# A linear-attention kernel with a feed-forward stage: four visits whose cross-half products go to PSUM banks of their own

## The chip, the core and the metric

The kernel runs on one core of a Trainium2 chip. TensorE (PE in the profile) multiplies matrices into PSUM, an accumulator of 8 banks, each of 512 float32 values on each of 128 partitions. VectorE (DVE), ScalarE (ACT) and GpSimd (POOL) do the element-wise work, and SyncE (SP) issues most of the loads and stores; GpSimd issues the weights' loads. The metric is the device time of one execution, in microseconds. Lower is better.

## What is computed

The first stage is causal linear attention with a decay. There are 4 batches, 8 heads, 768 positions and 64 channels; `lam` holds one decay per head. Position i attends to j <= i with weight `lam**(i-j)`, in blocks of 64 with a state between them:

```python
for b in range(nb):
    intra = einsum(qb, kb) * Dmask           # lam**(i-j) where i >= j
    intra = einsum(intra, vb)
    inter = einsum(qb * lam**(pos+1), kv_state)
    out[block] = intra + inter
    kv_state = lam**block * kv_state + einsum(kb * lam**(block-1-pos), vb)
```

The second stage takes these outputs as 3072 rows x of 512 and computes `h = x @ w_in` (512 to 2048), `g = h * cos(h)` and `g @ w_out` (2048 to 512). All inputs and the output are float32; the matmuls are done in bfloat16.

## The kernel before

**Blocks, visits and pairs.** The 3072 rows are 24 visits of 128 positions, each two halves of 64. Two visits of two batches make a pair. The first two pairs (visits 0 to 3, `SPANS`) are done at the start in another layout (`add_span`). Pairs 2 to 11 go through `prepare`, `add_scores` and `add_stretch`. Names such as q4 or v5 are loads for the visit of that number, so the loads of visits 4 and 5 are those of the third pair.

**One pair.** q and v are scaled by powers of `lam` (L341, L349), k is cast (L345). q and k are transposed, on TensorE for pair 2 and by a DMA for later pairs (L377). `scores` (L419) multiplies k with q into two banks ps_s, and VectorE masks them into s_m (L424). `update` (L431) adds up k times v into ps_kv, and VectorE and ScalarE make the running state from it (L437, L442). `values` and `values_carried` (L480, L508) make the output in two banks ps_o, one for each visit: first the "cross" products, in which half 0 of the array's rows works on visit 1 and half 1 on visit 0, then the "straight" ones, in which half s works on visit s, then the products with the carried state. `values_out` (L516) copies a bank to xT, the input of the feed-forward stage.

**Why there is a drain.** [...]between cross and straight products each half changes its bank. Where the scores of the next pair are put between the two groups, a small copy on VectorE (`turn`, L493) tells that the first group is over. Pairs 3 to 6 have their scores elsewhere (`ALONE = [3, 4, 5, 6]`), so behind pairs 2, 3, 4, 5 and 11 there is nothing to put between, and TensorE drains:

```python
def values_carried(_):
    if not more:
        nc.tensor.drain()
```

**The feed-forward stage.** `add_ffn` works on tiles of 4, 2, 2, 2, 2, 2, 2, 4 and 4 visits. For each of 16 column blocks f, `hidden` (L705) makes ps_h from xT and w_in, ScalarE its cosine (L711), VectorE the product g (L717). `project` (L749) multiplies g with w_out into ps_f, ScalarE copies that to o_sb (L763), and SyncE stores it.

**Order.** A planner in the kernel (`Planner`) puts all tasks in an order from costs that are written in the code, takes PSUM banks as they come free in its plan, and the program is recorded in that order. On the chip each engine goes through its own instructions in this fixed order and waits by semaphores. The order of loads is written out by hand (`ORDER`); `add_load` and `add_w` make each load wait for an earlier one where the list changes between weights and inputs:

```python
ORDER = "q0 k0 q1 k1 v0 v1 i0 i1 i2 i3 i4 i5 o0 o1 o2 q4 q5 k4 k5 o3"
deps = [kept[-3 if soft else -2]] if at and (names[at - 1][0] in "io") != soft else []
```

Here i0 to i5 are the pieces of w_in (`W_IN = [2, 2, 2, 4, 4, 2]` blocks f), o0 to o3 those of w_out. So q4 waits for the landing of o1, v4 for that of k5, and o3 for that of q4. i3 waits in addition for VectorE's first masked scores of the second span (`w_late`). GpSimd issues i0, i1 and i2 first, then scales k of the second span, then issues i3 and the rest. Until the main stage begins TensorE has filler matmuls (`keep_awake`).

Of the kernel before, what the change touches and what calls it, by code (L numbers as in the profile page):

```python
# [18 lines left out]
SPANS = 2  # L19
# [5 lines left out]
ATT = 0.95  # L25
LOAD_US = 1.22
ALONE = [3, 4, 5, 6]


QK = [{"q": ("DVE", "DVE"), "k": ("DVE", "DVE")}, {"q": ("DVE", "DVE"), "k": ("POOL", "POOL")}]  # L30
# [111 lines left out]
def kernel(  # L142
# [12 lines left out]
    P = 128  # L155
# [132 lines left out]
    def add_load(n, name, src, prio, deps=()):  # L288
        b, c = where(n)

        def emit(_):
            t = loads.tile([P, H, D], F32, tag=name, name=name)
            live[name, n] = t
            return start(nc.sync, t, src[b, :, c * P:(c + 1) * P, :].transpose([1, 0, 2]), deps)

        issue_t[name, n], load_t[name, n] = dma("SP", LOAD_US, 0.85, emit, prio, deps, get=name, lat=1.0)
        return load_t[name, n]

    w_t, w_late = {}, []

    def add_w(which, c, prio, deps=()):
        def emit(_):
            if which == "in":
                a, z = sum(W_IN[:c]) * P, sum(W_IN[:c + 1]) * P
                i = start(nc.gpsimd, w_in_sb[:, :, a:z], w_in_src[:, :, a:z], deps)
                if c == 3:

                    tc.add_manual_dep(i.ins, w_late[0].ins.ins.name, mybir.DependencyInfo(
                        mybir.DependencyClass.Sync, mybir.DependencyReason.DATA), reason="lines of instructions first")
                return i  # L310
            a, z = c * KF // WCH, (c + 1) * KF // WCH
            return start(nc.gpsimd, w_out_sb[:, a:z, :], w_out_src[:, a:z, :], deps)

        part = W_IN[c] / 4 if which == "in" else 1.0
        early = which == "in" and c < 3
        _, w_t[which, c] = dma("POOL", 2.68 * part, 0.8, emit, -2000.0 if early else prio, deps,
                               lat=1.2)
        return w_t[which, c]
# [151 lines left out]
    def add_stretch(pr):  # L470

        n0 = 2 * pr
        g, c = divmod(pr, NB)
        pa = lambda part: prio_attn(n0, part)
        tile_i, j0 = tile_of(n0)

        def value(s, half):
            m, o = halves[half], live["o", n0 + s]
            for h in range(H):
                yield lambda h=h: nc.tensor.matmul(  # L480
                    o[halves[h % 2], h // 2, m], lhsT=live["v_s", n0 + s][m, h, :], rhs=live["s_m", n0 + s][m, h, :],
                    start=(s != half and h < 2), stop=True, skip_group_check=True)

        def values(t):
            for s in range(2):
                live["o", n0 + s] = bank(t.bank[s], [P, NP, P], F32, "ps_o")
            for x, y in zip(value(1, 0), value(0, 1)):
                x()
                y()

        def turn(_):

            live["turn", pr] = nc.vector.tensor_copy(spare[D:D + 1, 0:1], live["o", n0][D:D + 1, NP - 1, D:D + 1])  # L493

        def values_carried(_):
            if not more:
                nc.tensor.drain()
            for x, y in zip(value(0, 0), value(1, 1)):
                i = x()
                y()  # L500
                if ("turn", pr) in live:
                    tc.add_manual_dep(i.ins, live.pop(("turn", pr)).ins.name, mybir.DependencyInfo(
                        mybir.DependencyClass.Sync, mybir.DependencyReason.DATA), reason="row halves in turn")
            for half in range(0 if c else 1, 2):
                S = live["S", pr, 0] if half else live["S", pr - 1, 1]
                for h in range(H):
                    for s, r in enumerate(halves):
                        nc.tensor.matmul(live["o", n0 + s][halves[h % 2], h // 2, halves[half]], lhsT=S[r, h, :],  # L508
                                         rhs=live["qkT", pr][r, 0, h, halves[half]],
                                         start=False, stop=True, skip_group_check=True)  # L510

        def values_out(_, s, e):
            if ("xT", tile_i) not in live:
                live["xT", tile_i] = work.tile([P, KD, 4 * P], BF16, tag="xT", name="xT")
            j = j0 + s
            (nc.vector.tensor_copy if e == "DVE" else nc.scalar.copy)(  # L516
                live["xT", tile_i][:, :, j * P:(j + 1) * P], live.pop(("o", n0 + s)))

        deps = [So[n0], So[n0 + 1], Uo[pr, 0], Uo.get((pr - 1, 1)) if c else None]
        more = pr + 1 < NBLK // 2 and pr + 1 not in ALONE  # L520
        v1 = pl.add("PE", 4 * QUART + SW, deps, values, pa(0.5), banks=2)
        chain = [v1]
        if more:
            nxt = list(add_scores(pr + 1, pa(0.5)))
            for t in nxt:
                v1.deps += [d for d in t.deps if d not in nxt]
            chain += nxt
        if more:
            deps = deps + [pl.add("DVE", 0.12, [v1], turn, pa(-9.0))]
        v2 = v12[pr] = pl.add("PE", (12 if c else 8) * QUART + (0.0 if more else 0.28), deps, values_carried, pa(0.5))  # L530
        chain.append(v2)
        v1.bank_frees = []
        for s in range(2):
            e = "DVE" if pr == SPANS and s == 0 else "ACT"
            Vo[n0 + s] = [pl.add(e, 0.65, [v2] + ([h_last[tile_i - 2]] if tile_i >= 2 else []), partial(values_out, s=s, e=e),
                                 pa(0.0 if e == "DVE" else 0.6))]
            v1.bank_frees.append(Vo[n0 + s])
            So[n0 + s].frees = [v2]
            v_head[n0 + s].frees = [v2]
        qkT_head[pr].frees = [v2]  # L540
        if (pr + 1, 1) in Uo:
            Uo[pr + 1, 1].deps.append(v2)
        for x, y in zip(chain, chain[1:]):
            x.then = y
            y.deps.append(x)
# [4 lines left out]
    def add_span(x):  # L550
# [77 lines left out]
        for hp in range(2):  # L628
            eq, ek = QK[x]["q"][hp], QK[x]["k"][hp]
            a = pl.add(eq, us[eq], [load_t["q_f", "sp", x]], partial(prep, name="q", hp=hp, e=eq), pa(-0.9 + 0.1 * hp))  # L630
            kt.append(pl.add(ek, us[ek], [load_t["k_f", "sp", x]], partial(prep, name="k", hp=hp, e=ek), pa(-0.9 + 0.1 * hp)))
            if x:
                w_t["in", 3].issue.deps.append(kt[hp])
            outs = []
            for name, src in (("qT", a), ("kT", kt[hp])):
                e = OUTS[x][name][hp]
                t = pl.add("PE", MM(P, 4), [src, s_first if name == "kT" else None], partial(transposes, name=name, hp=hp), pa(-0.5 + 0.1 * hp), banks=1)
                outs.append(pl.add(e, 0.58 if e == "ACT" else 0.42, [t], partial(transposes_out, name=name, hp=hp, e=e), pa(-0.5 + 0.1 * hp)))
                t.bank_frees = [[outs[-1]]]
            s1 = pl.add("PE", 0.42, outs, partial(scores, hp=hp), pa(0.1 + 0.1 * hp), banks=2)  # L640
            if x and hp == 0:

                spans[0]["values"].deps.append(s1)
                s_first = s1
            so[hp] = [pl.add("DVE", 0.69, [s1], partial(scores_out, hp=hp, i=i), pa(0.1 + 0.1 * hp + 0.05 * i)) for i in range(2)]
            s1.bank_frees = [[t] for t in so[hp]]
            if x and hp == 0:
                w_late.append(so[hp][0])

        u = pl.add("PE", 0.42, v_t + kt + [spans[0].get("carried")], update, pv(0.1), banks=1)  # L650
        Uo_sp[x] = [pl.add(e, 0.4 if e == "ACT" else 0.42, [u], partial(update_out, h=h, e=e), pv(0.1))
# [37 lines left out]
    def add_ffn(i):  # L689
# [4 lines left out]
        for f in range(KF):  # L694
            gate[f] = []
            blocks = [(0, 2), (2, 4)] if i == 0 and f < SPLIT else [(0, nb)]
            for b0, b1 in blocks:
# [16 lines left out]
                def gated(_, f=f, at=at, n=n):  # L714
                    if ("g", i) not in live:
                        live["g", i] = work.tile([P, KF, 4 * P], BF16, tag="g", name="g")
                    nc.vector.tensor_mul(live["g", i][:, f, at], live.pop(("h", i, f, at.start))[:, :n],  # L717
                                         live.pop(("c", i, f, at.start))[:, :n])

                h = pl.add("PE", MM(n, 4), [x for m in range(n0 + b0, n0 + b1) for x in Vo[m]] + [w_t["in", next(c for c in range(len(W_IN)) if f < sum(W_IN[:c + 1]))]],  # L720
                           hidden, pr, banks=1)
# [2 lines left out]
                h.bank_frees = [[d]]  # L724
                a.frees = [d]
                gate[f].append(d)
                h_last[i] = h
                if i == 0:
                    hid.append(h)
# [58 lines left out]
    for at, name in enumerate(names):  # L788
        which, n = name[0], int(name[1:])
        soft = which in "io"  # L790
        deps = [kept[-3 if soft else -2]] if at and (names[at - 1][0] in "io") != soft else []
        if name == "o3":
            deps = [load_t["q_f", 2 * SPANS]]
        if soft:
# [6 lines left out]
    idle = pl.add("SETUP", 0.0, [], None, -1e9, banks=1)  # L801
    for x in range(SPANS):
        add_span(x)
    w_t["in", 3].issue.deps += w_late
    add_span_state()
    for pr in range(SPANS, NBLK // 2):
        prepare(pr)
# [8 lines left out]
        add_ffn(i)  # L816
    for f in range(2, SPLIT):
        hid[2 * f].deps.append(spans[1]["carried"])
    closing.deps.append(v12[SPANS])
    first_sum.deps += Vo[2 * SPANS]  # L820
    lead_end = hid[2 * SPLIT]
# [55 lines left out]
```

## Time and profile before

| what | value |
|---|---|
| three runs | 205.86, 206.45 (median), 206.87 us |
| profiled run | 206.59 us, span of the core 204.8 us |
| PSUM to xT copy on ScalarE, 128x512 (L516) | 589 ns each, x19 |
| product g on VectorE, 128x256 and 128x512 (L717) | 503 ns mean, x148 |
| q, k and v loads of 256 KB, issue to landing | 3.8, 4.3, 4.7 us (median) |
| w_out pieces of 512 KB, issue to landing | 12.1 us (median) |

The span runs from the first to the last instruction of the profiled execution, and all times in the trace count from its start. In rows of a timeline the first number is the start, the second the length of the merged stretch, and "x32" how many instructions it holds; the bracket gives the idle time before it and what ended that. Matmuls overlap, so the lengths of neighbouring rows on TensorE can overlap too; distances between starts are the safer measure. A few matmul records are missing, which shows as a gap of one matmul's length.

### The profile page before, as it was taken

Reading aid. Unit: us, or ns where it says so; the run is one execution under the profiler, and the core shown is the slowest. Engines: PE = TensorE matmul, PEld = TensorE weight load, DVE = VectorE, ACT = ScalarE, POOL = GpSimd, SP = SyncE. Lnnn points to the kernel's source line nnn. Section 1 sums busy time; section 2 is a strip of 40 time slices with the busy share of each in tenths; the row PEclk is TensorE's granted clock in tenths of the full one; section 3 lists DMA queues with packets and bytes.
Section 4 is the critical chain, followed back from the end, with each engine's and each line's share of the span. In section 5 each row is a group of like instructions: output and inputs, shape, how many; then the busy total and the mean of one; then the engine's idle time right before and its main releaser. Section 6 shows DMA issues by size and latency. Waiting matters only on the chain.

```text
span 204.8 us, 5936 instructions
## 1 busy us (share of the span) xinstructions
PE 195.6 (95%) x2457; PEld 117.6 (57%) x2485; DVE 113.6 (55%) x221; ACT 119.2 (58%) x232; POOL 64.8 (32%) x85
## 2 busy tenths in 40 slices
PE   6999999999999999999999999999999999999993
PEld 2467444547747848666658666755454444444463
DVE  2887783347953947559467664735687444444001
ACT  5978771128837868466649586645778555354120
POOL 5865004064345362616364443436300000000000
PEclk9999999999999999999999999999999999999999
DMA  4999999999989998999999889989700110111112
GB/s 128 317 190 196 199 202 214 187 205 232 213 214 231 259 213 202 209 201 251 216 270 155 204 183 215 246 202 268 133 0 6 51 51 0 51 54 51 51 71 82
DMA packets 96906, 33.94 MB, mean 166 GB/s; under 512 B 84336, under 2 KB 93936, under 8 KB 96880
## 3 DMA queue, kind: packets, MB, share of 16 engines
q1 hardware_dynamic: 89376, 28.78, 62.0%
q0 software_dynamic: 7360, 4.72, 16.3%
q8 instruction: 19, 0.31, 0.6%
q10 hardware_dynamic: 144, 0.07, 0.1%
q14 instruction: 7, 0.06, 0.1%
HBM read 27.27 MB, written 6.29 MB: 164 GB/s over the span
## 4 chain that ended last, share of the span: by engine, by line
PE 76%; DMA 14%; SPq 3%; POOL 2%; issue 2%; DVE 1%; ACT 0%; POOLq 0%; ACTq 0%
PE ps_f L749 35%; PE ps_h L705 34%; DMA w_out_sb<-in_moe_w_out_dram 6%; DMA v_f<-in_v_dram 3%; DMA sp_f<-in_k_dram 3%; SPq L266 3%; PE ps_o L480 2%; DMA k_f<-in_k_dram 2%; PE ps_kv L431 2%; PE ps_o L508 1%; PE ps_s L419 1%; POOL w_in_sb L266 1%; POOL k_sp L564 1%; DVE v_s L349 0%; POOL w_out_sb L266 0%
## 5 line engine op out<-in xcount | busy, mean ns | idle before, releaser
L717 DVE TENSOR_TENSOR g<-ps_h,cos 128x256 bf16<-128x256 f32 (+1 forms) x148 | 73.0, 503 | 51.7 <-ACT cos L711 50.7
L711 ACT ACTIVATE cos<-ps_h,halfpi 128x256 f32<-128x256 f32 (+1 forms) x148 | 75.8, 539 | 31.3 <-PE ps_h L705 30.9
L705 PE MATMUL ps_h<-xT,w_in_sb 128*128 128x256 bf16 (+1 forms) x587 | 91.4, 304 | 0.6 <-issue 0.5
L749 PE MATMUL ps_f<-w_out_sb,g 128*128 128x512 bf16 (+2 forms) x393 | 88.5, 362 | 2.2 <-issue 1.4
L705 PEld LDWEIGHTS <-w_in_sb 128*128 128x128 bf16 x592 | 57.1, 98 | 31.2 <-issue 0.6
L749 PEld LDWEIGHTS <-g 128*128 128x128 bf16 x416 | 38.5, 98 | 35.7
L763 ACT COPY o_sb<-ps_f 128x512 f32<-128x512 f32 (+1 forms) x24 | 13.8, 574 | 29.8 <-PE ps_f L749 29.5
L341 POOL TENSOR_TENSOR qk<-q_f,q_scale 128x512 bf16<-128x512 f32 x19 | 19.7, 1045 | 34.5 <-DMA q_f<-in_q_dram 21.8
L349 POOL TENSOR_TENSOR v_s<-v_f,v_scale 128x512 bf16<-128x512 f32 x19 | 19.6, 1044 | 21.6 <-DMA v_f<-in_v_dram 19.2
L516 ACT CAST xT<-ps_o 128x512 bf16<-128x512 f32 x19 | 10.3, 589 | 11.4 <-PE ps_o L508 8.9
L424 DVE TENSOR_TENSOR s_m<-ps_s,mask 128x512 bf16<-128x512 f32 x20 | 12.9, 684 | 3.3 <-PE ps_s L419 3.0
L345 POOL CAST qk<-k_f 128x512 bf16<-128x512 f32 x18 | 11.0, 614 | 5.8 <-DMA k_f<-in_k_dram 5.7
L437 DVE TENSOR_TENSOR sum<-sum,ps_kv 128x512 f32<-128x512 f32 x15 | 10.2, 683 | 0.8
L442 ACT CAST S<-sum 128x512 bf16<-128x512 f32 x15 | 9.0, 616 | 0.8 <-DVE sum L437 0.7
L480 PEld LDWEIGHTS <-v_s 64*64 64x64 bf16 x320 | 4.3, 106 | 5.0 <-issue 4.4
L763 DVE COPY o_sb<-ps_f 128x256 f32<-128x256 f32 (+1 forms) x2 | 0.7, 358 | 11.2 <-PE ps_f L749 11.2
L480 PE MATMUL ps_o<-s_m,v_s 64*64 64x64 bf16 x320 | 6.4, 198 | 0.5
L837 PE MATMUL ps_idle<-blank 128*128 128x512 f32 (+2 forms) x8 | 5.3, 814 | 1.6 <-DVE blank L209 1.6
L588 DVE TENSOR_TENSOR s_m_sp<-ps_s,mask_sp 128x512 bf16<-128x512 f32 x8 | 5.1, 684 | 1.0 <-PE ps_s L583 1.0
L431 PE MATMUL ps_kv<-v_s,qk 64*64 64x64 bf16 x288 | 4.7, 194 | 0.4 <-DVE v_s L349 0.3
L266 POOL DMA_DIRECT2D w_in_sb<-in_moe_w_in_dram x6 | 4.6, 774 | 1.7 <-DVE s_m_sp L588 1.7
L679 POOL CAST S<-sum 128x512 bf16<-128x512 f32 x1 | 0.6, 607 | 13.0 <-DVE sum L676 13.0
(70 smaller groups left out, 79.3 us busy)
## 6 DMA issues: line engine op xcount, KB each, us to landing
q_f<-in_q_dram SPq DMA_DIRECT2D x20, 256.0 KB, 3.8
k_f<-in_k_dram SPq DMA_DIRECT2D x20, 256.0 KB, 4.3
v_f<-in_v_dram SPq DMA_DIRECT2D x20, 256.0 KB, 4.7
out_dram<-o_sb SPq DMA_DIRECT2D x19, 256.0 KB, 2.4
w_out_sb<-in_moe_w_out_dram POOLq DMA_DIRECT2D x4, 512.0 KB, 12.1
out_dram<-o_sb SPq DMA_DIRECT2D x9, 128.0 KB, 3.8
sp_f<-in_q_dram SPq DMA_DIRECT2D x2, 512.0 KB, 5.0
sp_f<-in_k_dram SPq DMA_DIRECT2D x2, 512.0 KB, 6.0
```

Source lines behind the costliest of these rows:

```text
L266: i = queue.dma_start(out=o, in_=x)
L341: vec[e].tensor_mul(new_qk()[:, 0, :, s], live.pop(("q_f", 2 * pr + s)), q_scale[:, c, :].unsqueeze(2).to_broadcast([P, H, D]))
L345: (nc.scalar.copy if early else nc.gpsimd.tensor_copy)(new_qk()[:, 1, :, s], live.pop(("k_f", 2 * pr + s)))
L349: vec[e].tensor_mul(live["v_s", 2 * pr + s], live.pop(("v_f", 2 * pr + s)), v_scale[:, c, :].unsqueeze(2).to_broadcast([P, H, D]))
L424: nc.vector.tensor_mul(t, live["s", pr][s], mask.unsqueeze(1).to_broadcast([P, H, D]))
L480: yield lambda h=h: nc.tensor.matmul(o[halves[h % 2], h // 2, m], lhsT=live["v_s", n0 + s][m, h, :], rhs=live["s_m", n0 + s][m, h, :], sta ...
L516: (nc.vector.tensor_copy if e == "DVE" else nc.scalar.copy)(live["xT", tile_i][:, :, j * P:(j + 1) * P], live.pop(("o", n0 + s)))
L705: nc.tensor.matmul(t[:, :n], lhsT=w_in_sb[:, kd, f * P:(f + 1) * P], rhs=live["xT", i][:, kd, at], start=(kd == 0), stop=(kd == KD - 1))
L711: nc.scalar.activation(c[:, :n], live["h", i, f, at.start][:, :n], AF.Sin, bias=halfpi)
L717: nc.vector.tensor_mul(live["g", i][:, f, at], live.pop(("h", i, f, at.start))[:, :n], live.pop(("c", i, f, at.start))[:, :n])
L749: nc.tensor.matmul(live["f", i, j, piece][:, :width], lhsT=live["g", i][:, f, j * P:(j + 1) * P], rhs=w_out_sb[:, f, part], start=(f == 0) ...
L763: (nc.scalar.copy if eng == "ACT" else nc.vector.tensor_copy)(o[:, :width], live["f", i, j, piece][:, :width])
```

## The change

It has three parts.

1. In pairs 3, 4, 5 and 11 (`APART`) the cross products go to two further banks, ps_x, and the drain is left out. ScalarE copies each ps_x bank to SBUF (`cross_out`), and the output of each visit leaves in two halves: the half with no cross product as a copy on ScalarE, the other as a sum of ps_o and the copied cross product on VectorE (`halves_out`). The pair takes four banks.
2. q4 waits for VectorE's product of block f = 13 of tile 0 instead of o1's landing, and v4 for k4's landing instead of k5's.
3. i2, the third piece of w_in, is issued by GpSimd behind k's scaling instead of ahead of it, and i3 no longer waits for the masked scores.

The core of the diff:

```diff
+APART = [3, 4, 5, 11]
...
-        def value(s, half):
-            m, o = halves[half], live["o", n0 + s]
+        def value(s, half, o=None):
+            m = halves[half]
+            o = live["o", n0 + s][:, :, m] if o is None else o
...
-                    start=(s != half and h < 2), stop=True, skip_group_check=True)
+                    start=(apart or s != half) and h < 2, stop=True, skip_group_check=True)
...
+            if apart:
+                cross = live["cross", pr] = [bank(i, [P, NP, D], F32, "ps_x") for i in t.bank[2:]]
-            for x, y in zip(value(1, 0), value(0, 1)):
+            for x, y in zip(value(1, 0, cross[0]), value(0, 1, cross[1])):
...
-            if not more:
+            if not more and not apart:
                 nc.tensor.drain()
...
+            if s == half:
+                nc.scalar.copy(x, o)
+            elif half or c:
+                nc.vector.tensor_add(x, o, live["cross_f", pr][half])
...
+            nc.scalar.copy(live["cross_f", pr][half], live["cross", pr][half])
...
-        v1 = pl.add("PE", 4 * QUART + SW, deps, values, pa(0.5), banks=2)
+        v1 = pl.add("PE", 4 * QUART + SW, deps, values, pa(0.5), banks=2 + 2 * apart)
...
-                w_t["in", 3].issue.deps.append(kt[hp])
+                w_t["in", 2].issue.deps.append(kt[hp])
...
-    w_t["in", 3].issue.deps += w_late
...
+        if name == f"q{2 * SPANS}":
+            deps = []
+        if name == f"v{2 * SPANS}":
+            deps = [load_t["k_f", 2 * SPANS]]
...
+                if i == 0 and f == KF - 3:
+                    pace.append(d)
...
+    issue_t["q_f", 2 * SPANS].deps += pace
```

In the built program the order on TensorE is the same up to pair 3; from there some groups of ps_h and ps_f change places around the visits. SyncE's order changes only from the loads of pair 8 on, where some stores stand one or two places earlier or later; on GpSimd only the third piece moves.

More of the change, by code (lines that the diff above doesn't have):

```diff
@@ L293, in emit @@
             live[name, n] = t
-            return start(nc.sync, t, src[b, :, c * P:(c + 1) * P, :].transpose([1, 0, 2]), deps)
+            i = start(nc.sync, t, src[b, :, c * P:(c + 1) * P, :].transpose([1, 0, 2]), deps)
+            if (name, n) == ("q_f", 2 * SPANS):
+                tc.add_manual_dep(i.ins, pace[0].ins.ins.name, mybir.DependencyInfo(
+                    mybir.DependencyClass.Sync, mybir.DependencyReason.DATA), reason="order of loads")
+            return i
         issue_t[name, n], load_t[name, n] = dma("SP", LOAD_US, 0.85, emit, prio, deps, get=name, lat=1.0)
         return load_t[name, n]
-    w_t, w_late = {}, []
+    w_t, pace = {}, []
     def add_w(which, c, prio, deps=()):
@@ L304, in emit @@
                 a, z = sum(W_IN[:c]) * P, sum(W_IN[:c + 1]) * P
[L305 to L310, printed above, removed]
+                return start(nc.gpsimd, w_in_sb[:, :, a:z], w_in_src[:, :, a:z], deps)
             a, z = c * KF // WCH, (c + 1) * KF // WCH
@@ L475, in add_stretch @@
         tile_i, j0 = tile_of(n0)
-        def value(s, half):
-            m, o = halves[half], live["o", n0 + s]
+        def value(s, half, o=None):
+            m = halves[half]
+            o = live["o", n0 + s][:, :, m] if o is None else o
             for h in range(H):
                 yield lambda h=h: nc.tensor.matmul(
-                    o[halves[h % 2], h // 2, m], lhsT=live["v_s", n0 + s][m, h, :], rhs=live["s_m", n0 + s][m, h, :],
-                    start=(s != half and h < 2), stop=True, skip_group_check=True)
+                    o[halves[h % 2], h // 2], lhsT=live["v_s", n0 + s][m, h, :], rhs=live["s_m", n0 + s][m, h, :],
+                    start=(apart or s != half) and h < 2, stop=True, skip_group_check=True)
         def values(t):
@@ L486, in values @@
                 live["o", n0 + s] = bank(t.bank[s], [P, NP, P], F32, "ps_o")
-            for x, y in zip(value(1, 0), value(0, 1)):
+            cross = [None, None]
+            if apart:
+                cross = live["cross", pr] = [bank(i, [P, NP, D], F32, "ps_x") for i in t.bank[2:]]
+            for x, y in zip(value(1, 0, cross[0]), value(0, 1, cross[1])):
                 x()
@@ L517, in values_out, with halves_out, cross_out @@
                 live["xT", tile_i][:, :, j * P:(j + 1) * P], live.pop(("o", n0 + s)))
+        def halves_out(_, s, half):
+            if ("xT", tile_i) not in live:
+                live["xT", tile_i] = work.tile([P, KD, 4 * P], BF16, tag="xT", name="xT")
+            o, i = live["o", n0 + s][:, :, halves[half]], (j0 + s) * P + half * D
+            x = live["xT", tile_i][:, :, i:i + D]
+            if s == half:
+                nc.scalar.copy(x, o)
+            elif half or c:
+                nc.vector.tensor_add(x, o, live["cross_f", pr][half])
+            else:
+                nc.vector.tensor_copy(x, live["cross_f", pr][half])
+        def cross_out(_, half):
+            live.setdefault(("cross_f", pr), {})[half] = toks.tile([P, NP, D], F32, tag=f"cross{half}", bufs=1, name=f"cross{half}")
+            nc.scalar.copy(live["cross_f", pr][half], live["cross", pr][half])
         deps = [So[n0], So[n0 + 1], Uo[pr, 0], Uo.get((pr - 1, 1)) if c else None]
         more = pr + 1 < NBLK // 2 and pr + 1 not in ALONE
-        v1 = pl.add("PE", 4 * QUART + SW, deps, values, pa(0.5), banks=2)
+        apart = pr in APART
+        v1 = pl.add("PE", 4 * QUART + SW, deps, values, pa(0.5), banks=2 + 2 * apart)
         chain = [v1]
@@ L529, in add_stretch @@
             deps = deps + [pl.add("DVE", 0.12, [v1], turn, pa(-9.0))]
-        v2 = v12[pr] = pl.add("PE", (12 if c else 8) * QUART + (0.0 if more else 0.28), deps, values_carried, pa(0.5))
+        v2 = v12[pr] = pl.add("PE", (12 if c else 8) * QUART + (0.0 if more or apart else 0.28), deps, values_carried, pa(0.5))
         chain.append(v2)
         v1.bank_frees = []
+        if apart:
+            after = [v2] + ([h_last[tile_i - 2]] if tile_i >= 2 else [])
+            copies = [pl.add("ACT", 0.42, after, partial(halves_out, s=s, half=s), pa(0.6)) for s in range(2)]
+            moved = [pl.add("ACT", 0.42, [v1], partial(cross_out, half=half), pa(0.55)) for half in range(2)]
+            sums = [pl.add("DVE", 0.4, after + [moved[1 - s]], partial(halves_out, s=s, half=1 - s), pa(0.0 if pr == SPANS else 0.59 - 0.01 * s)) for s in range(2)]
+            for s in range(2):
+                Vo[n0 + s] = [copies[s], sums[s]]
+            v1.bank_frees = [Vo[n0], Vo[n0 + 1], [moved[0]], [moved[1]]]
         for s in range(2):
+            So[n0 + s].frees = [v2]
+            v_head[n0 + s].frees = [v2]
+            if apart:
+                continue
             e = "DVE" if pr == SPANS and s == 0 else "ACT"
@@ L537, in add_stretch @@
             v1.bank_frees.append(Vo[n0 + s])
-            So[n0 + s].frees = [v2]
-            v_head[n0 + s].frees = [v2]
         qkT_head[pr].frees = [v2]
@@ L646, in add_span @@
             s1.bank_frees = [[t] for t in so[hp]]
-            if x and hp == 0:
-                w_late.append(so[hp][0])
         u = pl.add("PE", 0.42, v_t + kt + [spans[0].get("carried")], update, pv(0.1), banks=1)
@@ L716, in gated @@
                         live["g", i] = work.tile([P, KF, 4 * P], BF16, tag="g", name="g")
-                    nc.vector.tensor_mul(live["g", i][:, f, at], live.pop(("h", i, f, at.start))[:, :n],
-                                         live.pop(("c", i, f, at.start))[:, :n])
+                    return nc.vector.tensor_mul(live["g", i][:, f, at], live.pop(("h", i, f, at.start))[:, :n],
+                                                live.pop(("c", i, f, at.start))[:, :n])
                 h = pl.add("PE", MM(n, 4), [x for m in range(n0 + b0, n0 + b1) for x in Vo[m]] + [w_t["in", next(c for c in range(len(W_IN)) if f < sum(W_IN[:c + 1]))]],
```

## Prediction

> **What bounds the kernel now.** I read the totals of the page first, then the waits of TensorE, then the timeline of TensorE around two kinds of visit, then SyncE, GpSimd and VectorE between 29 and 45 us.
>
> ```profile
> PE 195.6 (95%) x2457; PEld 117.6 (57%) x2485; DVE 113.6 (55%) x221; ACT 119.2 (58%) x232; POOL 64.8 (32%) x85
> PEclk9999999999999999999999999999999999999999
> ```
>
> TensorE is busy for 95% of the span at full clock; the next engines have 58% and 55%. So only what removes TensorE time, or a wait of TensorE, can move the end. Its waits by releaser:
>
> ```profile
> PE ps_f L749 <- issue: 1.4, 9, 0.2
> PE ps_h L705 <- issue: 0.5, 2, 0.3
> PE ps_kv L431 <- DVE v_s L349: 0.3, 1, 0.3
> ```
>
> After the start, one wait has another engine behind it: ps_kv on v_s. No wait on xT or on a PSUM bank is there. But a drain is not listed as a wait; it shows as distance between instructions. The timeline of TensorE, pair 3 (with a drain) and pair 6 (without):
>
> ```profile
> 60.95 0.74 PE L480 MATMUL ps_o<-s_m,v_s 64*64 64x64 bf16 x32
> 61.52 0.46 PE L508 MATMUL ps_o<-qkT,S 64*64 64x64 bf16 x32
> ...
> 104.62 0.32 PE L480 MATMUL ps_o<-s_m,v_s 64*64 64x64 bf16 x16
> 104.77 0.43 PE L419 MATMUL ps_s<-qkT 64*64 64x64 bf16 x32
> 105.07 0.45 PE L431 MATMUL ps_kv<-v_s,qk 64*64 64x64 bf16 x32
> 105.34 0.34 PE L480 MATMUL ps_o<-s_m,v_s 64*64 64x64 bf16 x16
> 105.49 0.35 PE L508 MATMUL ps_o<-qkT,S 64*64 64x64 bf16 x16
> ```
>
> With the drain the 32 matmuls of L480 take 61.52 - 60.95 = 0.57 us from first start to the start of L508. Without, the two halves take 0.15 (104.62 to 104.77) and 0.15 (105.34 to 105.49), 0.30 together. A drain costs 0.27 us. Pair 4 has 74.08 to 74.64, pair 5 84.56 to 85.13, pair 11 156.31 to 156.87: 0.56 or 0.57 each time.
>
> The one real wait begins with the order of SyncE's queue (its timeline; start, duration, what):
>
> ```profile
> 29.86 0.99 SPq L266 DMA_DIRECT2D q_f<-in_q_dram  x2
> 30.90 2.23 SPq L266 DMA_DIRECT2D k_f<-in_k_dram  x2
> 36.39 0.99 SPq L266 DMA_DIRECT2D v_f<-in_v_dram  x2
> ```
>
> and ends, in the timeline of all engines, on VectorE and TensorE:
>
> ```profile
> 33.80 0.75 POOL L266 DMA_DIRECT2D w_out_sb<-in_moe_w_out_dram  x1 [1.92 <-DMA q_f<-in_q_dram]
> ...
> 43.01 0.80 DVE L349 TENSOR_TENSOR v_s<-v_f,v_scale 128x512 bf16<-128x512 f32 x1 [1.02 <-DMA v_f<-in_v_dram]
> 43.31 0.22 PE L431 MATMUL ps_kv<-v_s,qk 64*64 64x64 bf16 x2
> 43.86 0.44 PE L431 MATMUL ps_kv<-v_s,qk 64*64 64x64 bf16 x30 [0.33 <-DVE v_s L349]
> ```
>
> The 32 ps_kv matmuls start at 43.31, do two, and go on at 43.86, when v_s of visit 5 is done (43.81): 0.55 us, of which some 0.52 is loss. SyncE issued v4 only at 36.39, when k5 had landed (36.37; landings here are the trace's semaphore events).
>
> **What the Trainium skill says.** "TensorE: Matmul & The Clock Gate", section "Single matmul latency", puts the pipe's drain at about 175 ns plus the columns, some 0.20 us for 64 columns; the trace has 0.27, and I use that. "TensorEngine Tiling (Array Packing)", section "Key Properties", says a change of tiling mode drains the array; the visit's number of changes stays, so nothing is gained there. "DMA: Bandwidth & Descriptors", section "Queues, rings and completion order", says an engine takes its queues in turn. The trace disagrees: from 36.8 to 38.8 us, after v4 was issued, the weights' queue moved 318 packets and the loads' queue one. "Runtime: NRT & Kernel Launch", section "Instruction fetch mechanics", has instructions come in blocks of 16 KB by a DMA queue of their own, ahead of use; the page agrees (queue 8: 19 packets, 0.31 MB).
>
> **The change, part by part.**
>
> *Drains.* Four of five drains go (pairs 3, 4, 5, 11; pair 2 keeps its own): 4 x 0.27 = 1.08 us off TensorE. The matmuls are the same in number and shape, 16 of each visit into ps_x. The order on TensorE is otherwise the same but for ps_h and ps_f groups that change places. Bounds: 0 if something else ends last at every visit, 1.1.
>
> *Copies and sums.* Per pair, ScalarE loses two 128x512 copies (589 ns each, L516) and gains four of 128x256; no such copy is in the trace. Nearest rows: the 64x256 cast of L600 at 0.37, the 128x256 cosine at 0.47; I take 0.37. So +0.3 us (at worst +0.7). VectorE gains two sums of 128x256 at 0.42 (as L717 of that size): +0.84. Over four pairs ScalarE 1.2 to 2.8 and VectorE 3.4 us, on engines idle for over 80. What matters is when xT is ready. Pair 3: ScalarE began 0.25 us after the last L508 start (61.80 to 62.05), so the first cross copy begins at 61.10 + 0.25 = 61.35; second done 62.09, all four 62.83; VectorE's sums 62.14 to 62.98. Eight ps_f lie behind the visit, and ps_h, the first user of xT, started at 63.64 and would at 63.37. Margin 0.39 us; with copies of 0.47 still 0.14. Before, it was 63.64 - 63.12 = 0.52. Pair 4 has the same eight ps_f; after pairs 5 and 11 only ps_h of an older tile and ps_f follow. Cost 0, worst 0.1 at two pairs. The pair holds four banks instead of two, the last until 62.98 where before it was 63.12; behind the four copies on ScalarE stand cosines whose ps_h comes 2 us later. Cost 0; upper bound 0.3 per visit.
>
> *q4 and q5.* The first q load of pair 2 waits for VectorE's product f = 13 of tile 0 (28.88 to 29.57) instead of a w_out landing (29.84). SyncE's queue behind it is the rest of the third pair's loads; on GpSimd the last w_out piece waits for q4's landing, with qk and v_s of pair 2 behind it. All come 0.25 us earlier. The transposes of qk (35.68) start as soon as q5's scaling ends, so later loads would be paid in full; up to 0.25 earlier is a gain of nothing, as TensorE had no gap there.
>
> *v4 and v5.* They wait for k4 (landed 35.11) instead of k5, so they go out 1.25 us earlier, 1.5 with the 0.25 above. If they share the DMA engines with w_out's last piece, v5 lands before 42 and the 0.52 goes. If they still stand behind that piece, only about 0.25 of it goes. A loss: the w_out piece (landed 41.18, first used at about 42.4) is slowed by over 1.2 us. I take 0.43, bounds -0.3 to 0.52.
>
> *The third w_in piece.* GpSimd issues it at about 12.06, behind k's scaling, not at 9.02; the fourth no longer waits for VectorE's product (13.48) and goes at 12.8 instead of 13.77, the fifth, sixth and three w_out pieces about 1 us earlier. k's scaling itself waited 0.22 for its load and isn't sooner. The weights' queue has 256 KB pieces ahead until 15.39 and ran at about 195 GB/s without a gap, so pieces are ordered by bytes, not by issue. The third piece landed at 17.93 and is first used at 18.89. I take 0; bounds: 0 to +2.1 (landing later by the whole 3.04, less 0.96 of margin).
>
> Sum: 1.08 + 0.43 = 1.51 us off the profiled span of 204.8, so 203.3. That run took 206.59, within the three shown (205.86 to 206.87, median 206.45): 206.45 - 1.5 = 204.95.
>
> **Rivals.** *Half of it*: v4 still waits behind w_out, or a bank or xT wait takes 0.1 to 0.2 per visit. For: the loads' queue was silent for 2 us. Against: the margins above. Only the drains gives 206.45 - 1.08 = 205.4; less a wait of 0.2 at four visits 206.2. *Nothing*: TensorE runs 1 us ahead and meets transposed q and k later. They land 2.4 us ahead of their scores at the tightest (54.28 against 56.73, 90.14 against 92.56), so 1 us isn't enough: 206.4. *Slower*: the fourth w_in piece was held until 13.48, and now four pieces (1.5 MB) go out from 12.1 to 15.1 without a pause. TensorE's next 16 KB of instructions is served between 15 and 18 us. If it queues behind them as v4 did, TensorE stops: v4's path took 6.2 us against q's 3.9, so 2.3; behind the whole 1.5 MB at 195 GB/s 7.7. At 4 us the run has 206.45 + 4 - 1.5 = 208.9; from 2.6 us on it is over 0.5% slower. Against: that queue was full already in the kernel before, and the block came through. *It does not do what it says* can be excluded: in the built order ps_x, the sums and the moved issue are there.
>
> **How the numbers follow.** Measurement tells about 0.5%, 1.03 us (205.42 to 207.48), from no change. Full effect 0.60 at 204.95 (204.2 to 205.6); half 0.25 at 205.4 to 206.2; nothing 0.07; slower 0.08. Faster: nearly all of the first and half of the second, 0.70; same 0.22; slower 0.08. The range 204.1 to 206.5 takes in the nothing case and leaves out the slower one, some 0.05 beneath (TensorE also has an unexplained stop of 0.4 at 117.9, which a new order may lose) and 0.05 for losses at visits above 0.2.
>
> **What would show it.** Right: L480 to L508 in 0.30 us at pairs 3, 4, 5 and 11; no gap in ps_kv near 43; ps_h after pairs 3 and 4 without a wait on the sums; first ps_h at 15.1 as before. Wrong: a gap of TensorE between 15 and 22 us, a wait of ps_f on w_out near 42, or waits of ps_h or ps_x on VectorE or ScalarE.

## The result and the profile after

Six runs of the changed kernel took 204.49 to 205.35 us, median 204.77; six of the kernel before took 205.59 to 206.87, median 206.32. The ratio is 0.9935, with a 95% interval of 0.9910 to 0.9959: faster by 0.65%, or 1.34 us (0.85 to 1.86). The means, 206.24 and 204.88, give the same ratio; the medians alone differ by 1.55 us. A second set of runs on another occasion gave 0.9941 (0.9919 to 0.9963). The forecast was 204.95 us, in a range of 204.1 to 206.5. The profiled span went from 204.8 to 203.0 us.

The page after, totals:

```profile
PE 195.0 (96%) x2457; PEld 118.0 (58%) x2485; DVE 116.7 (57%) x229; ACT 119.8 (59%) x240; POOL 64.5 (32%) x85
```

TensorE is still what fills the span, with the same 2457 matmuls. VectorE has 3.1 us more, ScalarE 0.6: eight sums and sixteen copies for eight larger copies.

The timeline of TensorE after, pair 3 (start, length, what):

```profile
60.52 0.32 PE L483 MATMUL ps_x<-s_m,v_s 64*64 64x64 bf16 x16
60.67 0.30 PE L483 MATMUL ps_o<-s_m,v_s 64*64 64x64 bf16 x16
60.80 0.52 PE L515 MATMUL ps_o<-qkT,S 64*64 64x64 bf16 x32
61.47 0.81 PE L783 MATMUL ps_f<-w_out_sb,g 128*128 128x512 bf16 x3 [0.16 <-issue]
```

The 32 matmuls of cross and straight products now take 0.28 us up to L515 (0.57 before), but L515 takes a little longer. From the first product of the visit to the first recorded ps_f behind it, it was 60.95 to 62.13, 1.18 us, and is 60.52 to 61.47, 0.95: 0.23 us less. (In both traces the record of one ps_f ahead of that is missing.) It is 0.23 less at pairs 4, 5 and 11 as well.

The rows of ScalarE and VectorE after, by shape (count, sum, mean ns, idle before):

```profile
L532 ACT CAST xT<-ps_o 128x256 bf16<-128x256 f32 x8 | 3.1, 383 | 0.6 <-DVE xT L534 0.3
L540 ACT COPY cross<-ps_x 128x256 f32<-128x256 f32 x8 | 2.6, 375 | 0.7 <-PE ps_x L483 0.7
...
L534 DVE TENSOR_TENSOR xT<-ps_o,cross 128x256 bf16<-128x256 f32 x8 | 3.1, 422 | 2.9 <-PE ps_o L515 2.9
```

They cost what the nearest rows of before said. In pair 3 the last sum ended at 62.26 and the last copy at 62.33; ps_h followed at 63.0. Its waits show none on them. The waits of TensorE after:

```profile
PE ps_idle L875 <- DVE blank L211: 1.6, 1, 1.6
PE ps_f L783 <- issue: 1.3, 8, 0.2
PE ps_h L737 <- issue: 0.3, 2, 0.2
PE ps_t L606 <- POOL k_sp L598: 0.2, 1, 0.2
```

The wait of ps_kv on v_s is no longer listed, but it isn't quite gone. TensorE's weight loads and VectorE near 43 us, after:

```profile
43.14 0.11 PEld L433 LDWEIGHTS <-qk 64*64 64x64 bf16 x3 [0.42 <-issue]
43.43 0.32 PEld L433 LDWEIGHTS <-qk 64*64 64x64 bf16 x29 [0.18 <-issue]
...
42.57 0.80 DVE L351 TENSOR_TENSOR v_s<-v_f,v_scale 128x512 bf16<-128x512 f32 x1 [0.64 <-DMA v_f<-in_v_dram]
```

The first loads go at 43.14, the rest at 43.43, when VectorE has v_s of visit 5 (43.37). What is left of the loss is 0.25 us. Before it was 0.52, and another 0.11 ahead of it: the first ps_kv had waited for v_s of visit 4.

**Where the 1.81 us came from.** I set the starts of the small matmul groups of both traces against each other and subtracted the work that changed places. The main stage began 0.04 us later; the transposes of pair 2 at 35.6 came 0.09 earlier against that; the waits on v_s gave 0.11 and 0.26; the four visits 0.23 each, 0.92; and a stop of TensorE at 117.9 us that the kernel before showed in its profile is absent, 0.47. The sum is 0.04 - 0.09 - 0.37 - 0.92 - 0.47 = -1.81. Without the stop it is 1.34, as in the timed runs; with an interval of 0.85 to 1.86 us on their side, this agreement to the last digit is luck. The 0.09 is within what the start of the transposes scatters from trace to trace (see below).

### The profile page after: what moved, and what is told of

Its sections match the earlier page's. It is cut to its first block, busy times and chain, and to the rows that moved or that the text cites. A ratio compares the mean times of both kernels' runs of the same rounds, so it can differ in the third digit from the quotient of the medians.

```text
span 203.0 us, 5951 instructions
## 1 busy us (share of the span) xinstructions
PE 195.0 (96%) x2457; PEld 118.0 (58%) x2485; DVE 116.7 (57%) x229; ACT 119.8 (59%) x240; POOL 64.5 (32%) x85
## 4 chain that ended last, share of the span: by engine, by line
PE 84%; DMA 8%; SPq 2%; issue 2%; DVE 1%; POOL 1%; ACT 0%; POOLq 0%; ACTq 0%
PE ps_h L737 41%; PE ps_f L783 35%; DMA v_f<-in_v_dram 4%; DMA sp_f<-in_k_dram 3%; SPq L268 2%; DMA k_f<-in_k_dram 2%; PE ps_o L483 2%; PE ps_kv L433 2%; PE ps_o L515 2%; PE ps_s L421 1%; PE ps_o L643 1%; PE ps_kv L630 1%; POOL k_sp L598 1%; PE ps_x L483 0%; DVE v_s L351 0%
## 5 line engine op out<-in xcount | busy, mean ns | idle before, releaser
L523 ACT CAST xT<-ps_o 128x512 bf16<-128x512 f32 x11 | 6.0, 588 | 9.6 <-PE ps_o L515 6.3
L483 PEld LDWEIGHTS <-v_s 64*64 64x64 bf16 x320 | 3.9, 107 | 4.1 <-issue 3.6
L483 PE MATMUL ps_o<-s_m,v_s 64*64 64x64 bf16 x256 | 5.1, 196 | 0.1
L500 DVE COPY spare<-ps_o 1x1 f32<-1x1 f32 x5 | 0.8, 156 | 7.3 <-PE ps_o L483 7.3
L515 PE MATMUL ps_o<-qkT,S 64*64 64x64 bf16 x304 | 4.8, 194 | 0.0
```

Source lines behind the costliest of these rows:

```text
L483: yield lambda h=h: nc.tensor.matmul(o[halves[h % 2], h // 2], lhsT=live["v_s", n0 + s][m, h, :], rhs=live["s_m", n0 + s][m, h, :], start= ...
```

## The experiments

Ratios are to the kernel before, each with its 95% interval. One profile's span carries up to 0.7 us of difference in the start (the first transposes of the second span's k came between 11.12 and 11.85 us), so steps inside the trace count for more here than spans.

### One half and the other

`loads_only` has parts 2 and 3 of the change without the first:

```diff
-APART = [3, 4, 5, 11]
+APART = []
```

> The load and weight events of the change alone; no pair has banks of its own and all five drains stay, so TensorE's order is that of the kernel before. Theory (the gain is drains plus an earlier v): 0.09 at the first transposes and 0.37 at v_s come, 0.92 of drains does not: span 0.4 to 0.5 us below before, time 0.2% faster. Rival (the drains are hidden and the gain is the new order or the loads): most of the change's gain, 0.6% or more. L480 to L508 stays at 0.56 us in all five visits.

Measured: 0.9977 (0.9952 to 1.0001). L480 to L508 (L483 to L515 in this kernel) stays at 0.56 us. The theory's 0.2% fits, though the interval just takes in no change. Most of the gain, as the rival has it, did not come.

`apart_only` has part 1 alone; q4, v4, the third and the fourth w_in piece wait as before.

> Pairs 3, 4, 5 and 11 in banks of their own, all load and weight events as before. Theory: four visits shorter by 0.23 us each, the v_s wait of 0.6 us back at 43 us: 0.9 us below before, 0.45% faster. Rival (the gain is the new order of ps_h and ps_f, which loses the stop near 118 us): another 0.47 on top in every execution, 1.4 us or 0.7% faster. Rival (loads): no gain.

Measured: 0.9952 (0.9933 to 0.9971). Its four visits are 0.23 us shorter each, and the theory's 0.45% came. It shows no stop near 118 us. That it isn't 0.7% faster does not yet tell whether the stop is part of the usual time of the kernel before, since its wait on v_s is 0.6 us larger than there: 0.7 us ahead of the first ps_kv and 0.52 after the second. The product of the two ratios, 0.9952 x 0.9977 = 0.9929, agrees with the whole change.

### The drain itself

`drain_back` keeps banks, copies, sums and all orders of the changed kernel:

```diff
-            if not more and not apart:
+            if not more:
                 nc.tensor.drain()
```

> The changed kernel with the drain put back between the groups of pairs 3, 4, 5 and 11, while banks, copies, sums and every engine's order stay as changed. Theory (the drain itself is the cost, and the banks only allow its removal): each visit longer by 0.23 us, 0.9 us above the changed kernel, 0.2% to 0.25% faster than before. Rival (the shorter visit comes from separate banks as such): stays as fast as changed, 0.65%.

Measured: 0.9997 (0.9971 to 1.0024). The timeline of TensorE in this kernel, pair 3:

```profile
60.90 0.32 PE L483 MATMUL ps_x<-s_m,v_s 64*64 64x64 bf16 x16
61.37 0.32 PE L483 MATMUL ps_o<-s_m,v_s 64*64 64x64 bf16 x16 [0.15 <-issue]
61.51 0.46 PE L515 MATMUL ps_o<-qkT,S 64*64 64x64 bf16 x32
62.13 0.59 PE L783 MATMUL ps_f<-w_out_sb,g 128*128 128x512 bf16 x2 [0.16 <-issue]
```

The straight products start 0.47 us after the cross ones instead of 0.15, and the whole visit takes 1.23 us against 0.95: 0.28 for a drain, at each of the four pairs. So separate banks gain nothing as such; they allow the drain to go. With the drain in place the visit is even 0.05 us longer than in the kernel before, for a reason that stays open. The forecast of 0.2% to 0.25% faster than before lies within the interval.

In these kernels the drain, the scores put between the groups and the separate banks all serve one end: that the two row halves of the array don't write one bank at the same time. No run leaves out all three, so what would happen then is not shown.

### The kernel before once more

> The kernel before once more with a profile. If the stop of 0.47 us near 117.9 us belongs to its order, it is there again at the same instruction and the span is 204.8; if it is an event of one execution, it is absent or elsewhere and the span is 204.3 to 204.4.

Measured: one run of 207.46 us, span 205.7. From the waits of TensorE in this profile:

```profile
PE ps_h L705 <- issue: 0.8, 2, 0.6
```

The stop is there again, at 118.75 us in the same ps_h, and longer (0.77 us). Yet `loads_only`, `w_in_only` and `events_only`, whose order on TensorE is that of the kernel before, don't show it. So neither expectation holds: it is not bound to the order, and it isn't a single event either. In both profiles that have it a 16 KB block of instructions (queue 8) came late: it was through at 116.37 and 117.26, and the stop ended at 117.88 and 118.75, 1.5 us later each time. In the three others the block was through between 114.8 and 115.8, before the visit of pair 7 or with its start. That TensorE ran out of instructions there fits; no edit was made to show it.

The timed runs speak against a stop in every execution of the kernel before. Its profile, counted from the first transposes of the second span's k, is 1.15 us (0.56%) longer than that of `w_in_only`, stop included, but the timed runs of `w_in_only`, below, are only 0.05% to 0.43% faster. The same holds for the changed kernel: 1.81 us would be 0.88%, and its second set of runs has 0.37% to 0.81%.

### The events of the loads: what brought v earlier

`v_on_k5` is the changed kernel with v4 on k5's landing again:

```diff
-        if name == f"v{2 * SPANS}":
-            deps = [load_t["k_f", 2 * SPANS]]
```

> The changed kernel, but v4 waits for k5's landing again. Theory: v4 goes out 0.9 us later (35.7 instead of 34.8). Since it stood behind w_out's last piece (landed 40.8) until then, the landing moves by less than that: v5 lands 0 to 0.3 us later, the ps_kv wait near 43 grows from 0.25 to at most 0.55, 0 to 0.15% slower than changed. Rival (issue time sets landing): v5 lands 0.9 later and the wait is 1.1 us, 0.4% slower than changed.

Measured: 0.9917 (0.9886 to 0.9948). v4 was issued at 35.88 us instead of 34.82, and v5 landed at 42.40, where it had been 42.55; no wait on v_s is left. So the rival is out, and the theory's larger wait did not come either. Here the event that v4 waits for does not decide when it lands.

`w_in_back` is the changed kernel with part 3 undone:

> The changed kernel with the third w_in piece ahead of k's scaling and the fourth behind the masked scores again. Theory (the weights' queue is limited by bytes): landings of the weights within 0.6 us of the changed kernel's, TensorE's first 40 us the same to 0.1 us, time the same to 0.1%. Rival (the early issue hinders or helps the start): over 0.5 us either way before 30 us.

Measured: 0.9952 (0.9932 to 0.9972). The first 30 us are the same, but the waits of TensorE have v_s again:

```profile
PE ps_kv L437 <- POOL v_s L355: 0.4, 1, 0.4
PE ps_kv L437 <- DVE v_s L355: 0.3, 1, 0.3
```

By the starts, TensorE waits 0.50 us ahead of the first ps_kv and 0.52 behind the second: 0.75 us more than in the changed kernel. Both expectations missed this. The timed runs alone would not show it: their interval overlaps that of the changed kernel. A new theory was made of it: part 3, which I had put at nothing, is what brings v earlier, through the weights' queue. Three more kernels, and the changed one once more, tested it.

`w_in_only` is the kernel before with part 3 alone, `events_only` with part 2 alone, `no_events` the changed kernel without part 2. The edits are those hunks of the diff.

> The kernel before with the third part of the change alone: third w_in piece behind k's scaling, the fourth without its wait. New theory (this part closes the dip of the weights' queue near 16 us, so w_out's third piece, q4, the last w_out piece and v5 follow about 0.5 us earlier each): v5 lands about 0.5 us earlier against the start of TensorE's first transposes, the wait on v_s near 43 falls from 0.63 to about 0.2, 0.2% faster than before. Recorded prediction (this part costs and gives nothing): wait and time as before.

Measured: 0.9976 (0.9957 to 0.9995), and no wait on v_s.

> The kernel before with the second part of the change alone: q4 on VectorE's product, v4 on k4's landing. New theory: v4 goes out earlier but lands 0.9 us after the last w_out piece as before, so the wait on v_s stays at 0.6 or more and the time is as before. Recorded prediction: the wait falls by about 0.43, 0.2% faster.

Measured: 1.0000 (0.9975 to 1.0025). The timelines of SyncE and TensorE in `w_in_only`:

```profile
36.05 0.99 SPq L268 DMA_DIRECT2D v_f<-in_v_dram  x2
...
43.33 0.47 PE L429 MATMUL ps_kv<-v_s,qk 64*64 64x64 bf16 x32
43.74 1.04 PE L779 MATMUL ps_f<-w_out_sb,g 128*128 128x512 bf16 x4
```

and in `events_only`:

```profile
35.33 0.99 SPq L268 DMA_DIRECT2D v_f<-in_v_dram  x2
...
43.45 0.22 PE L437 MATMUL ps_kv<-v_s,qk 64*64 64x64 bf16 x2
44.00 0.44 PE L437 MATMUL ps_kv<-v_s,qk 64*64 64x64 bf16 x30 [0.33 <-DVE v_s L355]
```

Where v4 goes out later (36.05) the 32 ps_kv matmuls run through; where it goes out earlier (35.33) they stop for the same 0.52 us as before. The cause is upstream. Work by stretch (stretch, busy time and count of each engine, clock, DMA share, GB/s), before and then `w_in_only`:

```profile
16.00:17.00 1.00, 1.00 (x25) 0.77 (x24) 0.70 (x2) 0.80 (x3) 1.00 (x3) 1.00 1.18 154
```

```profile
16.00:17.00 1.00, 1.00 (x25) 0.69 (x24) 0.47 (x2) 0.91 (x2) 1.00 (x3) 1.00 1.35 202
```

Between 16 and 17 us the weights' queue, the only one with data there, moves 154 GB/s before and 202 with part 3. What follows is a chain: w_out's third piece, q4 behind it, the last w_out piece issued at q4's landing, v4 and v5 behind that.

All 14 profiles divide by part 3, and by it alone: five kernels lack it (the kernel before twice, `apart_only`, `events_only`, `w_in_back`) and nine have it. Times count from the first transposes of the second span's k; the dip is in the microsecond that begins 4.88 us after them.

| | five without part 3 | nine with part 3 |
|---|---|---|
| all DMA queues in the dip's microsecond | 143 to 157 GB/s | 202 to 208 GB/s |
| q4 landed | 21.9 to 22.2 us | 21.3 to 21.7 us |
| v5 landed (without `o3_on_k5`, 28.4) | 31.9 to 32.4 us | 30.6 to 31.5 us |
| first to last weight load of ps_kv (0.22: no wait) | 0.88 to 1.47 us | 0.22 to 0.64 us |

So part 3 is shown to be the cause; the links between the dip and v5 are read from the traces and were not forced one by one. Whether the earlier issue of the fourth piece or the place of the third closes the dip was not tried apart either.

> The changed kernel without its second part: q4 waits for w_out's second piece and v4 for k5 again. New theory: wait on v_s near 43 within 0.2 us of the changed kernel's, time within 0.1% of it. Recorded prediction: 0.43 us more wait, 0.2% slower than changed.

Measured: 0.9931 (0.9907 to 0.9956), no wait on v_s.

> The changed kernel once more, as a reference on the same chip: 0.65% faster than before, wait on v_s 0.2 to 0.4 us, no stop of TensorE near 117 us.

Measured: 0.9941 (0.9919 to 0.9963), no wait on v_s and no stop near 117 us. Part 2 gives nothing that can be measured, with or without the rest. If anything, the early v4 hurts a little: with part 3 in place, the three kernels that issue v4 late (`w_in_only`, `v_on_k5`, `no_events`) show no wait on v_s, while three of the five profiles that issue it early still show 0.25 to 0.4 us (changed kernel, `loads_only`, `drain_back`; `o3_on_k5` is left aside). These are single profiles, and the cause stays open.

### Is v held up by the last w_out piece?

`o3_on_k5`:

```diff
         if name == "o3":
-            deps = [load_t["q_f", 2 * SPANS]]
+            deps = [load_t["k_f", 2 * SPANS + 1]]
```

> The changed kernel, but w_out's last piece waits for k5's landing instead of q4's, 2.4 us later; the planner puts its four ps_f users further back. Theory (v stands behind this piece): v4 and v5 land by 39.5 us, the wait of ps_kv on v_s goes and 0.25 us with it, 0.1% faster than changed, unless a ps_f waits for the late piece. Rival (v is slow for another reason): v5 still lands at 42.5 and the wait stays.

Measured: 0.9979 (0.9949 to 1.0009). v5 landed at 39.84 us, 2.7 earlier than in the changed kernel, and ps_kv doesn't wait. The piece itself, issued at 36.87, landed at 44.72, and TensorE's timeline has the price:

```profile
44.76 1.46 PE L783 MATMUL ps_f<-w_out_sb,g 128*128 128x512 bf16 x6 [0.73 <-DMA w_out_sb<-in_moe_w_out_dram]
```

The escape that the expectation named came: a ps_f waits for the late piece. So v did stand behind that piece: in the other 13 profiles v4 never lands sooner than 0.88 us after it (0.88 to 0.92 in eight, 0.96 to 2.45 in five). Passing it moves the wait from v_s to w_out and makes it longer.

### The fifth drain

`pair2_apart`:

```diff
-APART = [3, 4, 5, 11]
+APART = [2, 3, 4, 5, 11]
```

> The changed kernel with pair 2 in banks of its own too, so that no drain is left. Theory: 0.23 us less at pair 2, 0.1% faster than changed, unless its xT comes late: behind this visit stand only four ps_f (0.86 us) before the first ps_h of tile 1, where the sums on VectorE end some 1.2 us after the visit, so 0.2 to 0.4 us of new wait: 0 to 0.1% slower than changed.

Measured: 0.9935 (0.9915 to 0.9955), the changed kernel's ratio. TensorE's timeline behind the visit of pair 2:

```profile
47.66 1.59 PE L737 MATMUL ps_h<-xT,w_in_sb 128*128 128x256 bf16 x13 [0.28 <-DVE xT L534]
```

The drain is saved and a wait on VectorE's sum takes its place, as expected, since here only four ps_f lie between the visit and the first ps_h. No version measurably beats the changed kernel; `v_on_k5` and `no_events` lie within its interval.

## Why the prediction was right, and where it was not

- **TensorE sets the end, and removing its own time moves it.** Right. What was taken off TensorE, 0.92 us at the four visits, came out of the span at full size.
- **Drains: 4 x 0.27 = 1.08 us.** The mechanism was right (`drain_back`), the term was too large: 4 x 0.23 = 0.92. I measured only up to L508. Up to there 0.29 went, but the products with the carried state take 0.06 longer to the next group; a visit without a drain, measured to the group behind it, would have told. The estimate of 0.20 us, from about 175 ns plus the columns in the Trainium skill's "TensorE: Matmul & The Clock Gate", "Single matmul latency", was 0.03 too low where mine was 0.04 too high.
- **Copies, sums and banks: nothing.** Right for the four pairs. Copies took 0.38 us, as taken from the 64x256 row, and the margin was 0.67 instead of 0.39. `pair2_apart` shows what a visit with half the cover pays.
- **v4 and v5 leave earlier: 0.43 us.** The size was near (0.37 came in the profile) by luck, as the step was wrong. `events_only` has the earlier issue and no gain, `v_on_k5` and `w_in_only` the later issue and no wait. The prediction saw the loads' queue silent behind w_out and took the earlier issue for a partial way round it; there was none.
- **The third w_in piece: 0.** Wrong. I held that the weights' queue ran "without a gap", so that pieces are ordered by bytes. The slice from 16 to 17 us, 154 GB/s against some 200 on both sides, was such a gap. Closing it is worth about 0.24% alone (0.05% to 0.43%), and this is the gain that I had written to the events.
- **q4's event, 0.25 us earlier for no gain.** Not shown. The transposes of pair 2 began 20.54 us behind the first ps_h before, 20.45 in the changed kernel and 20.45 in `w_in_only`, but 20.55 in `events_only`: the event alone brought nothing. All nine profiles with part 3 have 20.45, but two of the five without it have 20.45 or 20.46 too, so 0.09 us is within the scatter.
- **Signs.** Three of the four that were to show it right came: 0.28 us up to L515, no wait on the sums, the first ps_h at 15.2. The fourth, no gap in ps_kv, came in part: 0.25 us stayed in the first profile.
- **Rivals.** The times of "half of it" and "nothing" did not come. One condition of "half of it" did: v4 still waits behind w_out, and landed sooner only because part 3 moved the whole chain. "Slower", by instructions queued behind the weights, did not come at the start: the block of instructions went through at 15 us and TensorE has no gap between 15 and 22 us. Late instructions may cost something elsewhere, near 118 us, in the kernel before; the prediction had noted that stop as unexplained and left it outside the sum.

So the time was right because one term was too large by 0.16 us and another had, by luck, nearly the right size under the wrong name. From the timed runs alone this could not have been told.

## What to carry to other kernels

Where the critical engine drains between two groups that share banks, banks of their own for one group trade the drain for copies on engines with slack; check first how much other work lies between the group and the reader of the sum, because a visit with half the cover gave all of it back. When a load lands late, look at what is ahead of it in the DMA engines before moving its trigger: the transfer behind a long weight piece landed no sooner than 0.88 us after it, whether it was issued 1 us earlier or later. And read the throughput of a queue in slices as short as the effect that is at stake, before calling it gapless.

## What the runs showed of the hardware

A load of 256 KB issued on SyncE's queue while a 512 KB weight piece of GpSimd's queue was under way landed 0.88 to 0.92 us behind that piece in eight profiles, for issue times from 34.8 to 36.7 us, and 0.96 to 2.45 behind it in five more. That doesn't look like engines that take their queues in turn, which is what the Trainium skill says in "DMA: Bandwidth & Descriptors", "Queues, rings and completion order". It says so of queues that have work, though, and whether the load had packets ready all that time the traces don't tell.

Leaving out a drain of TensorE between two groups of 64x64 matmuls, with banks of its own for one group, shortened the visit by 0.23 us in all eight profiles that do so; putting it back there lengthened it by 0.28.
